# Long convolution and token mixing: the last 64 token rows in two column tiles of TensorE

## The chip, the cores and the metric

The kernel runs on one core of a Trainium2 chip. A core has five engines with their own instruction streams: TensorE (PE in the profile, its weight loads PEld), VectorE (DVE), ScalarE (ACT), GpSimd (POOL) and SyncE (SP). Data lies in HBM, in SBUF (128 partitions) and in PSUM, where TensorE puts its sums (128 partitions, eight banks of 512 float32 each). Transfers are issued from SP, ACT and POOL. The metric is the device time of one execution in microseconds (us), lower is better.

## What is computed

Two stages follow one another. The first is a long convolution of `x` (8 batches, 5696 tokens, 128 channels) with `h` along the tokens, by way of Fourier transforms. The second mixes tokens with two 5696 x 5696 matrices:

```python
x = irfft(rfft(x, n=2*S, axis=1) * rfft(h, n=2*S, axis=0), n=2*S, axis=1)[:, :S, :]
theta = x @ w_theta
zr, zi = x * cos(theta), x * sin(theta)
y = einsum('ts,bsd->btd', w_tok_r, zr) + einsum('ts,bsd->btd', w_tok_i, zi)
u = x + y
out = u + maximum(u @ w_ch, 0)
```

Batch and channel together are 1024 columns, so the mixing is a product of a 5696 x 11392 matrix (both weights side by side) with 11392 x 1024.

## The kernel before, in words

The first 570 us or so are the convolution, which doesn't change. What follows is the mixing.

**Tiles.** The 5696 token rows of the output are 44 tiles of 128 and one last tile of 64 (`NT - 1`, rows 5632 to 5695). The 1024 columns are two halves of 512, one PSUM bank each. The sum over 5696 input tokens is made in two passes (`p`), of 2816 tokens each (`H`), and 64 tokens left over, whose part is added in pass 1 by `zl` and `wl`. A pass takes its 2816 tokens in 11 blocks (`NJ`), each with a real and an imaginary half (`r`).

**Pairs and the seven products.** In a pass the 44 tiles go in pairs `tt` (tile `tt` with tile `22 + tt`). Most pairs are multiplied with Strassen's seven products, in banks `m0` to `m6` (named M2, M6, M7, M5, M1, M3, M4; line 1084 has the matmuls, line 1091 the adds on VectorE). For this, the z operand of each block `j` lies in SBUF as `bts[j]`, seven quarters of 512 columns: M2, M6, M7 and M5 begin as b11, b12, b21 and b22, and M3, M4, M1 (and M6, M7) become sums and differences of them (`sum_ops`, line 653, adds at line 655). The order of the pairs is 0 to 20, then the last tile alone (`None`), then 21 in pass 0, and 0, then the last tile, then 1 to 21 in pass 1. Pair 0 (and 1 in pass 0) is multiplied plainly (line 1005).

**The last tile.** It has 64 rows and can't be paired. Its product with b11, b12, b21, b22 is written in terms of the quarters that lie there:

```python
terms = ((sa, M2, a2, M4), (a1, M3, sa, M5))
```

`a1` and `a2` are the real and the imaginary weights of the tile, transposed, and `sa` their sum. Column half `h` = 0 is `sa` x quarter M2 plus `a2` x quarter M4; half 1 is `a1` x M3 plus `sa` x M5. For each block and `r` this makes four matmuls (lines 968 and 970), 128 deep, 64 rows out, 512 columns. Half 0 goes into one PSUM bank and half 1 into another, both on partitions 0 to 63.

**Stretches.** The 11 blocks are loaded in two chunks (6 and 5 blocks) and worked in four stretches of 3, 3, 3 and 2 blocks. For every stretch `prepare` transposes the weights on VectorE (line 714, into a pool of five buffers `wt`) and adds or subtracts them (line 723, into four buffers). It is called one stretch ahead. For the last tile a stretch needs two transposes and one sum.

**The ring of weights.** Weights come from HBM by transfers that POOL issues (line 509, four for each load) into a ring of six loads. A load may be issued when the load six places before it has been transposed to the end of its chunk.

**z between the passes.** Pass 1 needs other z blocks. `load_b` (line 639) reads them from `z_hbm`, two transfers for each block, issued on ACT, as soon as the block's buffer isn't needed by pass 0 any more; so these loads follow TensorE through pair 21. `start_pass(1)` then loads `zl` for the 64 left-over tokens (line 846, on SP) and adds its two halves (line 847).

**Sums and final stages.** In pass 0 the bank is added to an addend (`addend`: the convolution's output in bfloat16, `yy`, loaded on SP, line 826) and the float32 result stored to `cp_hbm` (`finish`, line 833). In pass 1 that is loaded again (line 828) and added (line 986 for the last tile), and `finish` appends a final stage (`u_stage`) to a list `spread`. Its first part copies to bfloat16 (line 791, ACT), transposes on TensorE (line 794, `utp`) and copies back (line 796); its second multiplies with `w_ch` (line 801, `v`), takes maximum and sum on VectorE (line 803) and stores to the output (line 805, SP). `aside` takes such stages from `spread` between the matmuls of later stretches, one in each stretch; in pass 1 also in the last tile's.

**What sets the order.** A scheduler orders most engines' instructions by data and buffers. From the start of pass 1 to its pair 1 (and from pair 0 to late in pair 2 of pass 0), VectorE keeps the order in which the code is written (`manual_schedule`, line 916). In the last tile's stretches of pass 1 that order is: transposes and sum of the next stretch, the final add of a `u_stage`, then three adds for each block (line 977).

Of the kernel before, what the change touches and what calls it, by code (L numbers as in the profile page):

```python
# [10 lines left out]
F32 = mybir.dt.float32  # L11
BF16 = mybir.dt.bfloat16
# [10 lines left out]
def kernel(  # L23
# [10 lines left out]
    nc = tc.nc  # L34
    B, S, D = x.shape
    assert D == 128
    P = 128
    NT = (S + P - 1) // P
# [12 lines left out]
    y2_hbm = y2_hbm_h.ap()  # L51
    cp_hbm = cp_hbm_h.ap()
# [66 lines left out]
    for p0, p1 in ((0, 80), (80, NB)):  # L119
        nc.gpsimd.dma_start(u_t[p0:p1, :N2 * D],  # L120
                            bass.AP(tensor=h.tensor, offset=h.offset + p0 * N2 * D,
                                    ap=[[N2 * D, p1 - p0], [1, N2 * D]]))
# [20 lines left out]
    def turns_of(pattern, base, lanes, m, per, quarter=None):  # L143

        n = 1
        for _, c in pattern:
            n *= c
        t = s2.tile([P, 11 * NB], F32, tag="turn", name="turn")[:m, :n]
        k = s2.tile([P, 11 * NB], F32, tag="whole", name="whole")[:m, :n]
        nc.gpsimd.iota(k, pattern=pattern, base=base, channel_multiplier=0,  # L150
                       allow_small_or_imprecise_dtypes=True)
        nc.gpsimd.tensor_scalar(t, k, lanes, 1.0 / per, op0=mult, op1=mult)
        if quarter is not None:
            quarter(t)
        nc.vector.tensor_scalar(k, t, MAGIC, None, op0=add)
        nc.vector.scalar_tensor_tensor(t, k, MAGIC, t, op0=ALU.subtract, op1=ALU.subtract)
        return t, k
# [12 lines left out]
    t, k = turns_of([[1, K1]], 0, lane[:NB, 1:2], NB, N1)  # L170
# [324 lines left out]
    def wl_room():  # L495
        ring["wl"] += 1
        return small((4 + ring["wl"] % 2) * P, P)

    def yt_room():
        return small(0, 4 * P).rearrange("p (b n) -> p b n", b=4)  # L500
# [59 lines left out]
    M2, M6, M7, M5, M1, M3, M4 = range(7)  # L560
# [92 lines left out]
    def sum_ops(bt):  # L653
        b11, b12, b21, b22 = (bt[q] for q in (M2, M6, M7, M5))
        return [lambda f=f, x=x: f(*x) for f, x in (  # L655
            (nc.vector.tensor_sub, (bt[M3], b12, b22)), (nc.vector.tensor_sub, (bt[M4], b21, b11)),
            (nc.vector.tensor_add, (bt[M1], b11, b22)), (nc.vector.tensor_add, (b12, b11, b12)),
            (nc.vector.tensor_add, (b21, b21, b22)))]
# [19 lines left out]
    mps = ctx.enter_context(tc.tile_pool(name="mps", bufs=1, space=bass.MemoryType.PSUM, reuse_waits="tile"))  # L678
# [29 lines left out]
    def half(z, ti, h):  # L708

        return z[ti].rearrange("p b d -> p (b d)")[:, h * 512:h * 512 + 512]  # L710
# [74 lines left out]
    def u_stage(ti, h, c, m):  # L785
        st = {}

        def first(tags=("misc", "misc", None)):
            st["tags"] = tags
            ub = ybp.tile([P, 4, D], BF16, tag="yb", name="ub")  # L790
            nc.scalar.activation(ub[:m].rearrange("p b d -> p (b d)"), c[:m], AF.Copy)  # L791
            utp = mps.tile([P, 4, P], BF16, tag=tags[0], name="utp")
            for b in range(4):
                nc.tensor.transpose(utp[:, b, :m], ub[:m, b, :], ident_bf[:m, :m])  # L794
            st["uts"] = uts = cp.tile([P, 4, P], BF16, tag=tags[2], name="uts") if tags[2] else yt_room()
            nc.scalar.activation(uts[:, :, :m], utp[:, :, :m], AF.Copy)  # L796

        def second():
            v = mps.tile([P, 512], F32, tag=st["tags"][1], name="v")
            for b in range(4):  # L800
                nc.tensor.matmul(v[:m, b * D:(b + 1) * D], st["uts"][:, b, :m], w_ch_sb,  # L801
                                 start=True, stop=True)
            nc.vector.scalar_tensor_tensor(c[:m], v[:m], 0.0, c[:m],
                                           op0=ALU.max, op1=ALU.add)
            nc.sync.dma_start(
                bass.AP(tensor=out.tensor, offset=out.offset + ti * P * D + 4 * h * S * D,
                        ap=[[D, m], [S * D, 4], [1, D]]),
                c[:m].rearrange("p (b d) -> p b d", b=4))
        return nothing, first, second

    tags, where_bg = {"n": 0}, {}

    def addend(p, k, ti, h, m=P):

        tag = f"c{k}"
        if p == 1:
            tag = ("c0", "c1", "c2", "c3", "red", "mag")[tags["n"] % 6]
            tags["n"] += 1
        c = cp.tile([P, 512], F32, tag=tag, name=f"c{k}")
        if p == 0 and ti in (22, 23):  # L820
            yT = cp.tile([P, 4, P], BF16, tag=f"yy{k}", name=f"yy{k}")
            nc.sync.dma_start(yT, yt_hbm[:, 4 * h:4 * h + 4, ti * P:ti * P + P])
            return c, yT
        if p == 0:
            yy = cp.tile([P, 512], BF16, tag=f"yy{k}", name=f"yy{k}")
            nc.sync.dma_start(yy[:m], half(y2_hbm, ti, h)[:m])
            return c, yy
        nc.sync.dma_start(c[:m], half(cp_hbm, ti, h)[:m])
        return c, c

    def finish(p, ti, h, c, m=P):
        if p == 0:
            nc.sync.dma_start(half(cp_hbm, ti, h)[:m], c[:m])
        else:
            spread.append(u_stage(ti, h, c, m))
# [78 lines left out]
    for i, (k, p, tt, j0, s0, nj) in enumerate(stretches):  # L914
# [17 lines left out]
        bts, zl = bts_of[p], zl_of[p]  # L932
# [7 lines left out]
        def aside(first_of, second_of):  # L940
            nonlocal second
            if first_of and spread and (p == 1 or (tt > 0 and not end_of_pair)):
                where_bg["tags"] = ("c2", "c3") if j0 + s0 == TJ else ("red", "mag")
                _, first, second = spread.pop(0)
                with tc.issue_after(sides["late"].ins) if p == 0 and tt == 1 else ExitStack():
                    first()
                    if len(spread) > 1:
                        spread[1][0]()
            if second_of and second is not None:
                second()  # L950
                second = None

        if tt is None:
            if p:
                aside(True, False)
            if first_of_pair:
                ps = [mps.tile([P, 512], F32, tag=f"m{q}", name=f"m{q}") for q in ((M1, M7) if p else (M3, M4))]
                cs = [addend(p, h, NT - 1, h, m=64) for h in range(2)]
            a1, a2, sa = a
            terms = ((sa, M2, a2, M4), (a1, M3, sa, M5))  # L960
            for j in range(nj):
                jj = j0 + s0 + j
                for r in range(2):
                    b = [x[:, r, :] for x in bts[jj]]
                    st_ = jj == 0 and r == 0
                    sp_ = jj == NJ - 1 and r == 1 and zl is None
                    for h, (x0, q0, x1, q1) in enumerate(terms):
                        nc.tensor.matmul(ps[h][:64], x0[:, j, :64, r], b[q0],  # L968
                                         start=st_, stop=False)
                        nc.tensor.matmul(ps[h][:64], x1[:, j, :64, r], b[q1],  # L970
                                         start=False, stop=sp_)
            if p:
                aside(False, True)
            if p == 1:
                for j in range(nj):
                    for op in sum_ops(bts[j0 + s0 + j])[2:]:
                        op()
            if end_of_pair:
                if zl is not None:
                    wl = wl_room()  # L980
                    nc.sync.dma_start(wl[:, :64], wl_hbm[:, NT - 1, :64])
                    for h in range(2):
                        nc.tensor.matmul(ps[h][:64], wl[:, :64], zl[h], start=False, stop=True)
                for h in range(2):
                    c, c0 = cs[h]
                    nc.vector.tensor_add(c[:64], c0[:64], ps[h][:64])
                    finish(p, NT - 1, h, c, m=64)
            continue
        classic = plain(p, tt)
        if first_of_pair and i:  # L990
# [1 line left out]
        if first_of_pair:  # L992
            where = ((tt, 1), (22 + tt, 0), (tt, 0), (22 + tt, 1))
            if zl is not None:
                wl = [wl_room(), wlp.tile([P, P], BF16, tag="wl1", name="wl1")]
                for n in range(2):
                    nc.sync.dma_start(wl[n], wl_hbm[:, 22 * n + tt, :])
        if j0 + s0 == (3 if classic else 2) * TJ:
            cs = (sides["cs"] if p == 0 and tt == 0 else
                  [addend(p, n, t, h) for n, (t, h) in enumerate(where)])  # L1000
# [33 lines left out]
        if classic:  # L1034
            for n in range(4):
# [4 lines left out]
                if end_of_pair and n % 2:  # L1040
                    (c12, z12), (c21, z21), (c11, z11), (c22, z22) = cs
                    out_of = (((c11, z11, 0), (c12, z12, 1)), ((c21, z21, 2), (c22, z22, 3)))[n // 2]
                    for h, (c, z, m_) in enumerate(out_of):
# [6 lines left out]
                        else:  # L1050
                            for b in range(4):
                                nc.tensor.matmul(ms[m_][:, b * D:(b + 1) * D], z[:, b, :], ident_bf,
                                                 start=False, stop=(b == 3))
# [11 lines left out]
        else:  # L1065
# [13 lines left out]
            for n, q in enumerate(ORDER):  # L1079
                sum_some(1)  # L1080
                for j in range(nj):
                    jj = j0 + s0 + j
                    for r in range(2):
                        nc.tensor.matmul(ms[q], a[q][:, j, :, r], bts[jj][q][:, r, :],  # L1084
                                         start=(jj == 0 and r == 0),
                                         stop=(jj == NJ - 1 and r == 1 and q not in left))
# [60 lines left out]
```

## Time and profile before

| | |
|---|---|
| median of 3 runs | 2110.66 us (2108.34 to 2111.68) |
| span of the profiled execution | 2116.2 us (nothing outside it is recorded) |
| busy in the span | PE 95%, DVE 76%, POOL 43%, ACT 32% |
| granted clock of TensorE, mean | 0.979 of full speed, 1.00 in the stretches of the last tile |
| last tile in pass 0 (lines 968, 970) | 1232.8 to 1251.8 us: 88 matmuls |
| pair 21, then start of pass 1 | from 1251.9 and from 1285.0 us |
| last tile in pass 1 | 1327.1 to 1351.2 us: 88 matmuls, 2 of line 983, three transposes `utp` and four products `v` of final stages |
| z of pass 1 read (line 639) | issued from 1259.0 to 1310 us, 8 to 19 us to landing |

The profile is one execution recorded instruction by instruction. Times count from the start of the span. A line of the timeline gives the start, the length, the engine, the code line, the operation, what it writes and reads, and in brackets how long the engine was idle before it and what ended that. Matmuls are pipelined: one of 512 columns is shown with 0.38 us, but the next can start 0.22 us after it, so the distance of starts is the cost of one in a row of many. "128\*64" is the part of the array in use: 128 rows deep, 64 columns.

### The profile page before, as it was taken

To read this page: it belongs to the slowest core of one execution; us is meant where nothing else is said; L and a number is where in the kernel's file an instruction comes from. 1 tells how busy PE (TensorE), PEld (TensorE's weight loads), DVE (VectorE), ACT (ScalarE), POOL (GpSimd) and SP (SyncE) were. 2 spreads that over 40 slices of the span, in tenths; PEclk is the share of its full clock that TensorE was granted. 3 is DMA by queue.
4 is the path that set the end of the run, shared out by engine and by line. 5 is a ranking of instruction groups with operands and counts; after the bars stand their busy time and mean duration, and the time that the engine had idled before them with its cause. 6 is when DMAs were issued, how large, how long until landed. Compare 5 with 4: busy or idle time off the path is not lost.

```text
span 2116.2 us, 41712 instructions
## 1 busy us (share of the span) xinstructions
PE 2008.1 (95%) x15873; PEld 1117.7 (53%) x15873; DVE 1598.3 (76%) x2884; ACT 673.9 (32%) x997; POOL 907.6 (43%) x1662
## 2 busy tenths in 40 slices
PE   4888999778999999999999999999999999999998
PEld 3788888654444444444444444444444444444444
DVE  7767776777778888888886755877777777776867
ACT  5778877774332333332310000111111111111111
POOL 5301010227444536354556543445454444545450
PEclk8799999999999999999999999999999999999999
DMA  6457474889989989898999879878888787979693
GB/s 140 98 130 170 117 180 127 216 245 243 178 153 179 176 176 168 170 176 173 174 165 156 142 137 296 128 117 147 140 143 145 134 153 128 156 127 157 124 156 90
DMA packets 408265, 334.97 MB, mean 158 GB/s; under 512 B 85927, under 2 KB 358439, under 8 KB 407079
## 3 DMA queue, kind: packets, MB, share of 16 engines
q0 software_dynamic: 225952, 156.72, 52.5%
q1 hardware_dynamic: 176128, 164.05, 27.3%
q10 hardware_dynamic: 5984, 11.54, 1.6%
q8 instruction: 124, 2.03, 0.4%
q14 instruction: 77, 0.63, 0.1%
HBM read 377.11 MB, written 92.49 MB: 222 GB/s over the span
## 4 chain that ended last, share of the span: by engine, by line
PE 68%; DMA 3%; DVE 3%; POOL 1%; issue 1%; ACT 0%; DVEq 0%; SPq 0%; POOLq 0%; ACTq 0%
PE m L1084 61%; PE m L1005 2%; DMA ring<-in_moe_w_tok_r_dram 1%; DMA b<-z_hbm 1%; POOL ring L509 1%; PE v L801 1%; PE utp L794 1%; DVE c L1091 1%; PE m L1088 1%; DVE b L655 1%; DVE wt L714 1%; DMA ring<-in_moe_w_tok_i_dram 0%; PE theta_ps L396 0%; PE tpz L742 0%; PE m L968 0%
## 5 line engine op out<-in xcount | busy, mean ns | idle before, releaser
L509 POOL DMA_DIRECT2D ring<-in_moe_w_tok_i_dram x720 | 387.9, 546 | 666.7 <-DVE wt L714 587.7
L714 DVE STREAM_TRANSPOSE wt<-ring 128x384 f32<-128x384 f32 (+2 forms) x720 | 360.5, 527 | 123.2 <-PE m L1084 71.3
L509 POOL DMA_DIRECT2D ring<-in_moe_w_tok_r_dram x720 | 386.4, 546 | 149.3 <-DVE wt L714 86.4
L1084 PE MATMUL m<-b,wt 128*128 128x512 bf16 x1640 | 388.3, 379 | 2.0 <-DVE wt L714 1.7
L1084 PEld LDWEIGHTS <-wt 128*128 128x128 bf16 x1804 | 175.8, 98 | 217.6 <-DVE wt L714 6.2
L1091 DVE TENSOR_TENSOR c<-c,m 128x512 f32<-128x512 f32 x412 | 266.9, 674 | 0.4 <-PE m L1084 0.4
L796 ACT ACTIVATE ring<-utp 128x512 bf16<-128x512 bf16 (+1 forms) x86 | 50.9, 592 | 586.2 <-PE utp L794 586.2
L328 PE MATMUL ps<-r_u,u_t 128*128 128x128 f16 x1024 | 128.6, 226 | 10.8 <-ACT red L419 5.6
L329 PE MATMUL ps<-r_v,v_t 128*128 128x128 f16 x1024 | 127.7, 226 | 0.4
L791 ACT ACTIVATE ub<-c 128x512 bf16<-128x512 f32 (+1 forms) x90 | 56.3, 628 | 215.0 <-DMA ring<-in_moe_w_tok_r_dram 123.8
L1005 PE MATMUL m<-b,wt 128*128 128x512 bf16 x480 | 112.9, 385 | 9.1 <-DVE wt L714 4.4
L130 POOL DMA_DIRECT2D x<-in_x_dram x64 | 33.9, 536 | 189.3 <-PE ps L194 177.8
L328 PEld LDWEIGHTS <-u_t 128*128 128x128 f16 x1024 | 104.1, 102 | 9.6 <-DVE u_t L312 6.2
L329 PEld LDWEIGHTS <-v_t 128*128 128x128 f16 x1024 | 103.4, 101 | 5.7 <-issue 3.2
L310 ACT ACTIVATE xs<-ps 128x1024 f16<-128x1024 f32 x96 | 95.9, 1023 | 15.1 <-DVE v_t L312 7.9
L312 DVE TENSOR_TENSOR u_t<-xs,hs 128x1024 f16<-128x1024 f16 x96 | 68.8, 716 | 32.1 <-ACT xs L310 19.7
L1005 PEld LDWEIGHTS <-wt 128*128 128x128 bf16 x528 | 50.8, 99 | 70.8 <-issue 8.7
L194 PE MATMUL ps<-f_t,x 89*128 89x180 f16 x512 | 77.2, 299 | 5.6 <-ACT xs L310 3.9
L212 PEld LDWEIGHTS <-w_t 64*128 64x128 f16 x3240 | 61.2, 102 | 34.8 <-issue 21.7
L398 ACT ACTIVATE red<-theta_ps,magic 128x512 f32<-128x512 f32 (+1 forms) x46 | 31.6, 687 | 133.7 <-PE theta_ps L396 116.0
L194 PEld LDWEIGHTS <-x 89*128 89x128 f16 x512 | 70.3, 241 | 6.6 <-issue 5.9
L744 ACT ACTIVATE ring<-tpz 128x512 bf16<-128x512 bf16 (+1 forms) x46 | 27.5, 597 | 132.6 <-PE tpz L742 108.9
(2914 smaller groups left out, 3916.7 us busy)
## 6 DMA issues: line engine op xcount, KB each, us to landing
ring<-in_moe_w_tok_r_dram POOLq DMA_DIRECT2D x352, 96.0 KB, 4.4
ring<-in_moe_w_tok_i_dram POOLq DMA_DIRECT2D x352, 96.0 KB, 5.0
ring<-in_moe_w_tok_r_dram POOLq DMA_DIRECT2D x352, 80.0 KB, 4.5
ring<-in_moe_w_tok_i_dram POOLq DMA_DIRECT2D x352, 80.0 KB, 3.9
hs<-hf_hbm SPq DMA_DIRECT2D x192, 128.0 KB, 3.2
cp_hbm<-c SPq DMA_DIRECT2D x88, 256.0 KB, 2.6
c<-cp_hbm SPq DMA_DIRECT2D x88, 256.0 KB, 4.4
out_dram<-c SPq DMA_DIRECT2D x88, 256.0 KB, 4.5
```

The costliest lines, as they stand in the source:

```text
L194: nc.tensor.matmul(ps[:, i // 2, (i % 2) * 2 * K1:(i % 2 + 1) * 2 * K1], lhs(q + i), f1_t[:NB], start=True, stop=True)
L212: nc.tensor.matmul(ps[:, e, j * HD:(j + 1) * HD], w_t2[rows, c0 + j, N2 * (1 - ri):N2 * (3 - ri)], a_st["a"][rows, ri * K1 + c0 + j, :], s ...
L310: nc.scalar.activation(xs[:, :, :, :ck], ps, AF.Copy)
L312: nc.vector.tensor_tensor(uv[r][:, :, :, c0:c0 + ck], xs[:, :, :, :ck], hv[:, r:r + 1, :, :ck].to_broadcast([P, 2, HD, ck]), op=mult)
L328: nc.tensor.matmul(o, u_t[:, at:at + P], r_u, start=True, stop=False)
L329: nc.tensor.matmul(o, v_t[:, at:at + P], r_v, start=False, stop=True)
L509: nc.gpsimd.dma_start(wb[32 * i:32 * i + 32, :ng, :nj * 64], bass.AP(tensor=a.tensor, offset=a.offset + row0 * S + p * H + i * QR + j0 * 6 ...
L714: nc.vector.transpose(wt.rearrange("p j t r -> p (j t r)").bitcast(F32).rearrange("p (j g t) -> p g j t", j=TJ, g=4)[:, :ng, :nj], wb[:, : ...
L791: nc.scalar.activation(ub[:m].rearrange("p b d -> p (b d)"), c[:m], AF.Copy)
L1005: nc.tensor.matmul(ms[n // 2 * 2 + h], a[n][:, j, :, r], bts_of[p][jj][n % 2 * 2 + h][:, r, :], start=(n % 2 == 0 and jj == 0 and r == 0), ...
L1084: nc.tensor.matmul(ms[q], a[q][:, j, :, r], bts[jj][q][:, r, :], start=(jj == 0 and r == 0), stop=(jj == NJ - 1 and r == 1 and q not in left))
L1091: nc.vector.tensor_tensor(c, z, ms[q], op=op)
```

## The change

The two column halves of the last tile go into one PSUM bank, half 0 on partitions 0 to 63 and half 1 on 64 to 127. TensorE then takes half 0's weights into its columns 0 to 63 and half 1's into 64 to 127. Matmuls of the two halves go by turns (first terms of both halves, then second terms). There is one accumulator, one addend `c_last`, one add of 128 partitions, and one store to `cp_hbm`, which uses the whole 128 rows of the last tile's place there (rows 64 to 127 hold half 1). In pass 1 one final stage of 128 partitions takes the place of two of 64; its result is stored by two transfers, one for each half.

```diff
@@ u_stage, second
-            nc.sync.dma_start(
-                bass.AP(tensor=out.tensor, offset=out.offset + ti * P * D + 4 * h * S * D,
-                        ap=[[D, m], [S * D, 4], [1, D]]),
-                c[:m].rearrange("p (b d) -> p b d", b=4))
+            for h_, p0, p1 in (((0, 0, 64), (1, 64, P)) if ti == NT - 1 else ((h, 0, m),)):
+                nc.sync.dma_start(
+                    bass.AP(tensor=out.tensor, offset=out.offset + ti * P * D + 4 * h_ * S * D,
+                            ap=[[D, p1 - p0], [S * D, 4], [1, D]]),
+                    c[p0:p1].rearrange("p (b d) -> p b d", b=4))
@@ new
+    def addend_last(p):
+        tag = "c0"
+        if p == 1:
+            tag = ("c0", "c1", "c2", "c3", "red", "mag")[tags["n"] % 6]
+            tags["n"] += 1
+        c = cp.tile([P, 512], F32, tag=tag, name="c_last")
+        if p == 0:
+            yy = cp.tile([P, 512], BF16, tag="yy0", name="yy_last")
+            for h in range(2):
+                nc.sync.dma_start(yy[64 * h:64 * h + 64], half(y2_hbm, NT - 1, h)[:64])
+            return c, yy
+        nc.sync.dma_start(c, half(cp_hbm, NT - 1, 0))
+        return c, c
@@ the last tile
-                ps = [mps.tile([P, 512], F32, tag=f"m{q}", name=f"m{q}") for q in ((M1, M7) if p else (M3, M4))]
-                cs = [addend(p, h, NT - 1, h, m=64) for h in range(2)]
+                q = M1 if p else M3
+                ps = mps.tile([P, 512], F32, tag=f"m{q}", name=f"m{q}")
+                c_last = addend_last(p)
...
-                    for h, (x0, q0, x1, q1) in enumerate(terms):
-                        nc.tensor.matmul(ps[h][:64], x0[:, j, :64, r], b[q0],
-                                         start=st_, stop=False)
-                        nc.tensor.matmul(ps[h][:64], x1[:, j, :64, r], b[q1],
-                                         start=False, stop=sp_)
+                    for k_ in range(2):
+                        for h, t in enumerate(terms):
+                            nc.tensor.matmul(ps[64 * h:64 * h + 64], t[2 * k_][:, j, :64, r], b[t[2 * k_ + 1]],
+                                             start=st_ and k_ == 0, stop=sp_ and k_ == 1)
...
-                        nc.tensor.matmul(ps[h][:64], wl[:, :64], zl[h], start=False, stop=True)
-                for h in range(2):
-                    c, c0 = cs[h]
-                    nc.vector.tensor_add(c[:64], c0[:64], ps[h][:64])
-                    finish(p, NT - 1, h, c, m=64)
+                        nc.tensor.matmul(ps[64 * h:64 * h + 64], wl[:, :64], zl[h], start=False, stop=True)
+                c, c0 = c_last
+                nc.vector.tensor_add(c, c0, ps)
+                finish(p, NT - 1, 0, c)
```

## The prediction

> **What bounds the kernel now.** I read the chain of waits on the page first, then the busy times of the two stretches in which the 64 rows are worked on, then the order of time inside them.
>
> ```profile
> PE 68%; DMA 3%; DVE 3%; POOL 1%; issue 1%; ACT 0%; DVEq 0%; SPq 0%; POOLq 0%; ACTq 0%
> 1232.80:1251.90 19.10, 19.10 (x90) 9.58 (x90) 7.53 (x19) 0.00 (x0) 8.57 (x16) 1.00 0.73 131
> 1327.00:1351.50 24.50, 23.36 (x122) 10.87 (x119) 22.89 (x44) 3.94 (x7) 9.36 (x18) 1.00 0.73 121
> ```
>
> The first line is the share of the chain by engine: TensorE (PE) holds 68% of what ended last. The other two are the stretches of pass 0 and pass 1 in which lines 968 and 970 run (columns after the length: PE, weight loads, VectorE (DVE), ScalarE, GpSimd (POOL), clock, DMA). In pass 0, PE is busy all 19.10 us and DVE 7.53: PE sets the end. In pass 1, DVE is busy 22.89 of 24.50 us: there PE has company, and the gain must be read from DVE.
>
> ```profile
> 1232.76 0.41 PE L968 MATMUL m<-ring,out__17787 128*64 128x512 bf16 x1
> 1232.78 0.11 PEld L970 LDWEIGHTS <-wt 128*64 128x64 bf16 x1
> 1233.00 0.38 PE L970 MATMUL m<-ring,wt 128*64 128x512 bf16 x1
> 1233.21 0.38 PE L968 MATMUL m<-ring,wt 128*64 128x512 bf16 x1
> ...
> 326.81 0.52 PEld L212 LDWEIGHTS <-w_t 64*128 64x128 f16 x32
> 326.81 0.64 PE L212 MATMUL ps<-a__6421,w_t 64*128 64x64 f16 x32
> ```
>
> Starts of matmuls lie 0.2157 us apart (88 from 1232.76 to 1251.74), whether or not they use half of the array's columns. A weight load of 64 columns (0.11 us) runs while a matmul streams. The last two lines are another stage, where matmuls go by turns to two halves of the array's rows: 32 of 64 columns in (0.64 - 0.19)/31 = 14.5 ns each. A full-array matmul of 128 columns comes every 56 ns in the same trace (line 328), so one of 64 would alone take some 28: two halves do work at once on this chip, with their loads. Two column halves are not in the trace.
>
> **The change, part by part.** Pass 0 and pass 1 each have 88 such matmuls, in stretches of 24, 24, 24 and 16. They become 44 pairs, one of each pair in array columns 0-63 and the other in 64-127. If a pair takes the time of one matmul, the four stretches take 12, 12, 12 and 8 x 0.2157 = 2.59, 2.59, 2.59 and 1.73 us instead of twice that. Bounds of a pair: 0.216 us (both at once, as L212) and 0.431 (by turns, as now); with both loads outside, 0.431 + 2 x 0.109 = 0.65. I take 0.216, the nearest row being L212.
>
> A rule of the Trainium skill ("TensorE: Matmul & The Clock Gate", Part 3, packing small matmuls) speaks against this: a weight load overlaps running matmuls only where the row group differs. Column halves share all rows, so by that rule a pair would take some 0.22 + 2 x 0.11 = 0.43 us and nothing would be won; the L970 load above, which starts 20 ns after a matmul in the same rows, speaks against it. The same part has three column tiles 2.38 times as fast as one after the other; as an estimate, two at that efficiency (0.79) would make a pair 0.27 us and take about 2 us from the gain below.
>
> *Pass 0.* What is late next is DVE:
>
> ```profile
> 1230.69 4.87 DVE L1091 TENSOR_TENSOR c<-c,m 128x512 f32<-128x512 f32 x8
> 1235.46 0.90 DVE L714 STREAM_TRANSPOSE wt<-ring 128x192 f32<-128x192 f32 x3
> 1236.28 0.32 DVE L723 TENSOR_TENSOR out__17845<-wt 128x384 bf16<-128x384 bf16 x1
> ```
>
> DVE adds the sums of the tile pair before until 1235.5, then transposes the weights of the second stretch and adds them (ready 1236.60). Today the first stretch lasts to 1237.9 and hides that. With 2.59 us it ends at 1235.35, and PE waits 1.3 us. Then 12 + 12 + 8 pairs: 1236.66 + 32 x 0.2157 = 1243.56, against 1251.74: **8.2 us** earlier. Later stretches find their weights: DVE's 4.4 us waits on L970 (for the five weight buffers) shrink, and it needs about 0.9 us for two transposes and a sum in each 2.59. The single sum of 128 rows comes ahead of w21's transpose in the order in which DVE's instructions are built, and the next pair's M3 bank waits for it: sum at 1243.8 to 1244.5 (0.67 us, row L986), while PE has four matmuls of M4 (0.86 us) first; if the next load of weights lands late (issued by POOL at 1236.1 to 1238.3, 4 to 5 us to landing), PE loses some 0.3. On SP one store of 128 rows takes the place of two of 64, and in pass 1 one load that of two: it has less to do, and nothing new is queued behind a wait there, since the two loads of the bf16 addend stay two and wait for the same buffer as before.
>
> The time won must pass through what follows. The next pair is PE's alone (1251.9 to 1285, no idle), then pass 1 needs z:
>
> ```profile
> 1250.00:1255.00 5.00, 5.00 (x24) 2.19 (x23) 3.46 (x7) 0.00 (x0) 0.00 (x0) 1.00 0.18 45
> 1255.00:1260.00 5.00, 5.00 (x25) 2.29 (x24) 3.65 (x9) 0.00 (x0) 3.98 (x8) 1.00 0.78 141
> 1265.00:1270.00 5.00, 5.00 (x25) 2.25 (x23) 2.84 (x6) 0.00 (x0) 2.71 (x5) 1.00 1.16 295
> 1290.00:1295.00 5.00, 5.00 (x25) 2.26 (x24) 0.09 (x1) 0.00 (x0) 0.00 (x0) 1.00 1.16 309
> ```
>
> DMA (share in the last column but one) is full, at 1.16, from 1265 to 1315, because z_hbm is read from 1259 on, as PE frees each b tile. PE then waits twice, 1.7 us at 1295 (zl, queued on SP behind b loads) and 1.2 at 1318. The b loads start 8 us earlier too. Does DMA have room? The 5 us shares from 1235 to 1315 sum to 15.9, so 79 us; at 1.16 that is 68 us of the 80. 11.7 us are free, mostly the hole at 1245 to 1260 that the earlier start closes. Four ring loads stay at 1236 to 1245 and may push into it. I take 0.5 us lost (bounds 0 and all 8.2, if b's landing did not move). Pass 0: 8.2 - 0.3 - 0.5 = **7.4 us**.
>
> *Pass 1.*
>
> ```profile
> 1331.09 0.36 DVE L723 TENSOR_TENSOR out__18603<-wt 128x384 bf16<-128x384 bf16 x1
> 1332.95 0.69 DVE L803 SCALAR_TENSOR_TENSOR c<-v,c 128x512 f32<-128x512 f32 x1 [1.50 <-PE v L801]
> 1340.51 5.50 DVE L655 TENSOR_TENSOR b<-b 128x1024 bf16<-128x1024 bf16 x9
> ...
> 1363.07 0.59 PE L1084 MATMUL m<-ring,out__18787 128*128 128x512 bf16 x2 [0.51 <-DVE c L986]
> ```
>
> DVE's order is fixed there. Each stretch costs it nine adds of b (5.5 us), two transposes and a sum (1.0) and a final add (0.69): 7.2 us, more than PE's 5.2. So halving PE wins one thing only: the final add at 1332.95 waits for v, behind the first stretch's matmuls; v will be there at 1330.5, and the add follows the sum at 1331.45: **1.5 us**. From there DVE runs without a gap to L986 at 1362.34. That sum then exists once instead of twice, and the built order puts six more matmuls ahead of the bank it frees: the 0.51 us wait goes. In the place of two final stages of 64 rows (utp 0.22 and v 0.34 each) comes one of 128 (0.22 + 0.22, as other pairs show): 1.12 - 0.44 = 0.68 us of PE. Pass 1: 1.5 + 0.5 + 0.7 = **2.7 us**; bounds 0 (if v is late for another reason) and 3.4 (0.67 us for the DVE sum on the path too). The two stores of 64 rows remain two and end 700 us before the kernel does.
>
> Sum: 7.4 + 2.7 = 10.1 us. The profiled span of 2116.2 becomes 2106.1. The runs' median is 5.5 us below that span, so I take the same off it: 2110.66 - 10.1 = **2100.6 us** (-0.48%).
>
> **Rivals.**
> - *By turns after all.* The two halves never overlap: a pair stays 0.431. For it: no row shows two column halves, and both read 128 rows of different moving data. Against it: L212. Left are the wait of 0.5 and the final stage's 0.7: 2109.4 us.
> - *Half hidden.* One load in each pair is exposed: 0.216 + 0.109 = 0.325 us. Pass 0 wins 44 x 0.106 = 4.7 (no DVE wait, since the first stretch then ends at 1236.66), less 0.5; pass 1 1.1 + 1.2: 2104.2 us. For it: the 64-column load takes 0.109, a full one 0.098. Against it: two such loads at 1232.75 and 1232.78 start 30 ns apart.
> - *Swallowed by DMA.* The pairs overlap, but b and zl land when they did, and pass 0 gives only what is left of the waits: 2110.66 - 2.7 = 2108.0 at the end of it; half of it, 2104.3. For it: 1.16 for 50 us. Against it: the hole before, and that the reads start when PE frees b.
> - *Slower: loads that stop the array.* If a load into one column half must wait until the other half's matmul is out, each of 88 matmuls pays 0.109 us: +9.6 us in pass 0, and in pass 1 PE (24.1 + 9.6) passes DVE, which sets that stretch now (7.2 x 3 + 5): about +7. 2110.66 + 16.6 - 1.2 = 2126 us. It decides from a pair above 0.46 us, where 44 x 0.03 eats the 1.2. For it: nothing shows a load beside a matmul in another column half. Against it: loads run beside matmuls everywhere else.
>
> **How the numbers follow.** Forecast 0.66, half hidden 0.10, swallowed 0.08, by turns 0.10, slower 0.06. The forecast's own range is 2097 (8.2 kept whole and 3.4, with 1.7 us of spread of the runs) to 2103.5 (2 us more lost in DMA, 1 in pass 1). To leave out no more than 2 in 10, I go up to 2107, past half hidden and half swallowed; by turns and slower stay out. 0.2% is 4.2 us, about what a measurement tells from no change: below 2106.4 is faster. Forecast, half hidden and a part of swallowed: 0.78; the rest of swallowed and by turns 0.15; slower 0.07.
>
> **What would show it.** In the profile after: pairs of matmuls starting some ns apart, the next pair 0.216 us later; 64-row stretch of pass 0 about 11 us long with one idle time of 1.3 us on DVE's sum; the first full-array matmul after it near 1243.7; z reads from about 1251; PE's waits near 1287 and 1310 no longer than 2 us; in pass 1 the stretch about 1.5 us shorter only, DVE at over 95%. Matmuls 0.216 apart would make it by turns; an unmoved zl landing, swallowed.

## The result, and the profile after

Over 20 runs the changed kernel took a median of **2102.05 us**, against 2111.72 us for the kernel before over 20 runs on the same chip: a ratio of **0.9954** (95% interval 0.9944 to 0.9964), or 9.7 us less (7.6 to 11.8). Forecast were 2100.6 us and 10.1 us less. The profiled run after took 2099.89 us with a span of 2098.1 us, 18.1 us below the span before; half of that difference is not the change, as the table of stretches below shows.

Pass 0 first: TensorE's order of time in the profile after, where the 64 rows begin (start, duration, engine, line, operation, output <- inputs, count, wait and who ended it).

```profile
1226.72 0.40 PE L986 MATMUL m<-ring,out__17787 128*64 128x512 bf16 x1
1226.72 0.62 PE L986 MATMUL m<-ring,wt 128*64 128x512 bf16 x2
1226.96 0.59 PE L986 MATMUL m<-ring,out__17787 128*64 128x512 bf16 x2
1227.18 0.59 PE L986 MATMUL m<-ring,wt 128*64 128x512 bf16 x2
...
1229.12 0.38 PE L986 MATMUL m<-b,out__17787 128*64 128x512 bf16 x1
1230.61 0.40 PE L986 MATMUL m<-b,out__17845 128*64 128x512 bf16 x1 [1.11 <-DVE out__17845 L723]
```

Lines 968 and 970 have become line 986. Matmuls now start in twos: two at 1226.72, then two in every 0.2157 us (1226.96, 1227.18; a line with x2 holds two, 0.2157 us apart). The stretch of 24 matmuls that took 5.2 us takes 2.6, and then TensorE waits for VectorE's sum: 1.11 us as listed, and 1.27 us from start to start beyond the usual 0.2157 (1229.12 to 1230.61), the wait that the prediction put at 1.3. The weight loads of the two halves stand in the same trace:

```profile
1226.71 0.11 PEld L986 LDWEIGHTS <-out__17787 128*64 128x64 bf16 x1 [0.42 <-DVE c L1106]
1226.72 0.14 PEld L986 LDWEIGHTS <-wt 128*64 128x64 bf16 x2
1226.75 0.32 PEld L986 LDWEIGHTS <-out__17787 128*64 128x64 bf16 x2
1226.96 0.32 PEld L986 LDWEIGHTS <-wt 128*64 128x64 bf16 x2
```

A load for one column half runs while the other half's matmul, which reads the same rows, is streaming. The rule that the prediction weighed against this (the Trainium skill, "TensorE: Matmul & The Clock Gate", Part 3: only a load into another row group overlaps, though the part elsewhere excepts a load into a background weight buffer) does not hold here. Busy times in the whole stretch (length; busy PE, weight loads, VectorE, ScalarE, GpSimd; granted clock; DMA share; GB/s):

```profile
1226.70:1237.60 10.90, 9.79 (x89) 4.88 (x88) 7.13 (x18) 0.00 (x0) 7.27 (x14) 1.00 0.89 178
```

19.10 us have become 10.90, with as many matmuls. VectorE does as much as before, so its share has gone from two fifths to two thirds.

In pass 1 it is VectorE that has to be read. Its order of time after the change:

```profile
1314.24 0.36 DVE L723 TENSOR_TENSOR out__18598<-wt 128x384 bf16<-128x384 bf16 x1
1314.52 0.68 DVE L803 SCALAR_TENSOR_TENSOR c<-v,c 128x512 f32<-128x512 f32 x1
1315.12 1.89 DVE L655 TENSOR_TENSOR ring<-ring 128x1024 bf16<-128x1024 bf16 x3
1316.92 3.69 DVE L655 TENSOR_TENSOR b<-b 128x1024 bf16<-128x1024 bf16 x6
```

The add of v (line 803) follows the weight sum at once: the wait of 1.50 us at 1332.95 is gone. The way from the last tile's first matmul to pair 1's first, before and after, in the view of busy times:

```profile
1327.14:1353.31 26.17, 23.27 (x120) 10.83 (x119) 24.57 (x47) 3.94 (x7) 9.22 (x18) 1.00 0.76 125
```

```profile
1310.30:1334.87 24.57, 15.30 (x120) 6.76 (x119) 24.47 (x47) 3.94 (x7) 9.31 (x18) 0.93 0.81 133
```

TensorE lost 8 of its 23 us, and the stretch lost 1.60: VectorE is busy 24.47 of 24.57. And the granted clock, 1.00 before, is 0.93. TensorE's waits and the clock around them, after:

```profile
1314.66 0.41 PE L986 MATMUL m<-b,out__18598 128*64 128x512 bf16 x1 [1.25 <-DVE out__18598 L723]
1321.61 0.63 PE L986 MATMUL m<-b,out__18655 128*64 128x512 bf16 x1 [3.18 <-DVE out__18655 L723]
1328.37 0.41 PE L986 MATMUL m<-b,out__18717 128*64 128x512 bf16 x1 [1.58 <-DVE out__18717 L723]
1335.24 0.63 PE L1099 MATMUL m<-ring,wt 128*128 128x512 bf16 x1 [3.63 <-DVE wt L714]
```

The last of these rows is not pair 1's first matmul: the trace lacks the record of that one, as it does in several runs, and of pair 21's first too. The weight loads show both, each with the load of a further matmul behind it:

```profile
1237.64 2.27 PEld L1099 LDWEIGHTS <-wt 128*128 128x128 bf16 x12 [0.41 <-DVE out__17950 L723]
1334.87 0.11 PEld L1099 LDWEIGHTS <-wt 128*128 128x128 bf16 x2 [3.55 <-DVE wt L714]
```

In the runs that have these two records, each stands within 0.02 us of its load (in the kernel before, 1251.87 and 1353.31 for both). So pair 1 starts at 1334.87, and the wait before it is 3.26 us, not 3.63.

```profile
1321.60:1325.00 3.40, 3.39 (x19) 1.36 (x20) 3.40 (x6) 0.60 (x1) 0.00 (x0) 0.54 0.46 133
1325.00:1328.30 3.30, 1.79 (x17) 0.78 (x13) 3.27 (x9) 0.00 (x0) 0.21 (x1) 1.00 0.29 79
1335.24:1338.60 3.36, 3.36 (x9) 1.30 (x9) 3.33 (x8) 0.00 (x0) 1.03 (x2) 0.54 0.19 59
1338.60:1342.00 3.40, 3.40 (x18) 1.51 (x17) 2.55 (x6) 0.00 (x0) 3.40 (x8) 1.00 1.03 125
```

Around the waits of 3.18 and 3.26 us the clock falls: it is 0.50 from 1321.29 to 1324.70 and from 1334.94 to 1338.35, 3.41 us each time (9 full-array matmuls are listed in 3.36 us, and 18 in the next 3.40). After those of 1.25 and 1.58 it does not fall.

All eleven profiles of this study by stretches, in us. "Start" is the first matmul of the 64 rows in pass 0; "64 rows, pass 0" goes from there to the first weight load of pair 21; "plain" from the first matmul of plain pair 0 in pass 1 to the first of the 64 rows; "64 rows, pass 1" from there to pair 1's first weight load. The other starts and ends are first matmuls in TensorE's order of time. (By first matmuls shown, five kernels with column tiles would have 11.15 or 11.16 us in pass 0 and the kernel after 24.94 in pass 1: that is the missing record and no time.)

| kernel | start | 64 rows, pass 0 | plain | 64 rows, pass 1 |
|---|---|---|---|---|
| before | 1232.76 | 19.11 | 41.97 | 26.17 |
| after | 1226.72 | 10.92 | 39.41 | 24.57 |
| column tiles in pass 0 only | 1230.07 | 10.92 | 40.39 | 26.17 |
| column tiles in pass 1 only | 1229.43 | 19.11 | 41.01 | 24.57 |
| one half after the other | 1222.01 | 13.66 | 40.69 | 25.34 |
| clock kept up | 1231.45 | 10.93 | 40.07 | 24.58 |
| 9 sums moved | 1225.89 | 10.92 | 40.20 | 21.63 |
| 18 sums moved | 1226.82 | 10.93 | 40.00 | 18.58 |
| kernel before, 18 sums moved | 1225.99 | 19.11 | 40.48 | 24.60 |
| 27 sums moved | 1225.56 | 10.92 | 39.75 | 14.48 |
| half 1 left out of pass 0 | 1227.72 | 10.92 | 42.12 | 24.57 |

The start varies from 1222.0 to 1232.8 although every kernel has the same code up to there: of the 18.1 us between the two spans, 6.0 come from it. The "plain" column varies by as much as 2.7 us, with the waits for late weights in it, and not with the change (39.4 to 42.1 with column tiles in pass 0, 40.5 to 42.0 without). The two stretches of 64 rows repeat within a few hundredths of a microsecond (10.92 or 10.93 in seven kernels; 24.57 or 24.58 in four). They are where this case can be read.

### The profile page after: what moved, and what is told of

Same layout as the page of the kernel before. It is cut to its first block, busy times and chain, and to the rows that moved or that the text cites. A ratio compares the mean times of both kernels' runs of the same rounds, so it can differ in the third digit from the quotient of the medians.

```text
span 2098.1 us, 41505 instructions
## 1 busy us (share of the span) xinstructions
PE 1979.5 (94%) x15688; PEld 1109.4 (53%) x15865; DVE 1595.2 (76%) x2881; ACT 675.3 (32%) x995; POOL 912.5 (43%) x1662
## 4 chain that ended last, share of the span: by engine, by line
PE 63%; DVE 4%; DMA 2%; issue 2%; POOL 0%; ACT 0%; DVEq 0%
PE m L1099 59%; DVE c L1106 2%; DMA ring<-in_moe_w_tok_r_dram 1%; DVE b L655 1%; PE v L801 1%; PE utp L794 1%; PE m L1103 1%; DVE wt L714 1%; PE tpz L742 0%; PE theta_ps L396 0%; POOL ring L509 0%; PE m L986 0%; DMA yT<-yt_hbm 0%; PE m L1020 0%; DMA zl<-zl_hbm 0%
## 5 line engine op out<-in xcount | busy, mean ns | idle before, releaser
L1099 PE MATMUL m<-b,wt 128*128 128x512 bf16 x1599 | 385.9, 380 | 4.1 <-DVE wt L714 1.7
L796 ACT ACTIVATE ring<-utp 128x512 bf16<-128x512 bf16 x85 | 50.8, 597 | 582.3 <-PE utp L794 582.3
L1020 PE MATMUL m<-b,wt 128*128 128x512 bf16 x466 | 110.2, 381 | 8.9 <-DMA b<-z_hbm 4.9
L791 ACT ACTIVATE ub<-c 128x512 bf16<-128x512 f32 x88 | 55.0, 628 | 191.5 <-DMA ring<-in_moe_w_tok_r_dram 113.0
L212 PEld LDWEIGHTS <-w_t 64*128 64x128 f16 x3240 | 60.8, 102 | 37.5 <-issue 24.5
```

What stands on the lines that cost most here:

```text
L212: nc.tensor.matmul(ps[:, e, j * HD:(j + 1) * HD], w_t2[rows, c0 + j, N2 * (1 - ri):N2 * (3 - ri)], a_st["a"][rows, ri * K1 + c0 + j, :], s ...
L1020: nc.tensor.matmul(ms[n // 2 * 2 + h], a[n][:, j, :, r], bts_of[p][jj][n % 2 * 2 + h][:, r, :], start=(n % 2 == 0 and jj == 0 and r == 0), ...
```

## The experiments

**Each pass alone.** The places in which the new form is chosen were made to depend on the pass; the first is shown, and matmuls, sums, loads and stores follow it:

```diff
-                q = M1 if p else M3
-                ps = mps.tile([P, 512], F32, ...)
+                if p == 0:        # in the second run: p == 1
+                    q = M1 if p else M3
+                    ps = mps.tile([P, 512], F32, ...)
+                    c_last = addend_last(p)
+                else:
+                    ps = [mps.tile(...) for q in ((M1, M7) if p else (M3, M4))]
+                    cs = [addend(p, h, NT - 1, h, m=64) for h in range(2)]
```

> Column tiles in pass 0 only; pass 1 works the last tile as the kernel before. Theory (pass 0 gives nearly all, because PE alone sets that stretch): 88 matmuls in about 10.9 us as in the changed kernel, 8 us won there, and all of it or a little more (the waits at the start of pass 1) kept: 8 to 10 us under the kernel before, ratio 0.9955 to 0.9965. Rival (both passes give alike, as both have the same 88 matmuls): 5 us, ratio 0.9975.

> Column tiles in pass 1 only. Theory (DVE sets that stretch, so only the 1.5 us wait for v and half a final stage can go): 1 to 3 us under the kernel before, ratio 0.9987 to 0.9995; the stretch of the last tile 1 to 2 us shorter, PE idle in it, clock below 1.00 in some slices of it as in the changed kernel. Rival (alike): 5 us, ratio 0.9975. If the two waits of PE at the start of pass 1 (1.7 and 1.2 us) are gone here too, their going has nothing to do with pass 0.

Pass 0 alone took 2104.35 us, ratio 0.9959 (0.9945 to 0.9973); pass 1 alone 2111.01, ratio 0.9990 (0.9976 to 1.0005), which can't be told from no change. In us below the kernel before: 8.7 (5.7 to 11.6) and 2.1 (-1.1 to 5.1), together 10.8 where the change has 9.7. These go by the ratios; the medians alone (2111.35 for the kernel before on that chip) differ by 7.0 and 0.3. The stretches don't depend on that choice: 8.2 us shorter in the one, 1.6 in the other. Most of the gain is pass 0.

**One half after the other.** In each stretch all matmuls of half 0 come first, then all of half 1; bank, sum and final stage stay those of the change.

```diff
-            for j in range(nj):
...
+            for h, t in enumerate(terms):
+                for j in range(nj):
...
-                    for k_ in range(2):
-                        for h, t in enumerate(terms):
+                        for k_ in range(2):
```

> The changed kernel's bank, sum, addend, stores and final stage, but in each stretch all matmuls of column half 0 and then all of half 1, so that two neighbours seldom lie in different halves. Theory (the gain is the two halves at work at once): pairs gone, the last tile in pass 0 takes some 18.5 to 19 us again, ratio 0.999 to 1.000. Rival (the gain is from one bank, one sum and one final stage, or from the order of transfers): ratio stays at 0.9954.

2102.94 us, ratio 0.9960 (0.9945 to 0.9975). By the theory this kernel should have lost the gain of pass 0, and it kept most of it. Nor is that the gain of one bank, one sum and one final stage without any overlap, for TensorE's order of time in that run shows the halves overlapping still:

```profile
1222.01 0.41 PE L986 MATMUL m<-ring,out__17787 128*64 128x512 bf16 x1
...
1223.54 0.38 PE L986 MATMUL m<-b,wt 128*64 128x512 bf16 x1
1223.76 0.38 PE L986 MATMUL m<-b,out__17787 128*64 128x512 bf16 x1
1223.77 0.40 PE L986 MATMUL m<-ring,wt 128*64 128x512 bf16 x1
1223.97 0.38 PE L986 MATMUL m<-b,wt 128*64 128x512 bf16 x1
1224.01 0.38 PE L986 MATMUL m<-ring,out__17787 128*64 128x512 bf16 x1
```

The matmul at 1223.77 reads "ring", the first block: it is half 1's first, thirteenth in the program, and it starts beside half 0's ninth. The stretch took 13.66 us: 5.4 below 19.11, where four overlapping matmuls at each of the seven changes of half in four stretches would give 7 x 4 x 0.2157 = 6.0. So taking turns is not what makes two column halves run together. It makes them do so all the time: 10.92 us.

**Half 1 left out.** In pass 0, 43 of half 1's 44 matmuls are left out; the kernel's output for these rows lacks them.

```diff
                         for h, t in enumerate(terms):
+                            if p == 0 and h and not (st_ and k_ == 0):
+                                continue
```

> The changed kernel with half 1 left out of the last tile's sum in pass 0, but for its first matmul: 44 matmuls and one in place of 88, all in one column tile (its output is not the reference's there). Theory (the second column tile costs nothing beside the first): the stretch from the first of these matmuls to pair 21's first stays at 10.9 to 11.2 us, with the matmuls 0.216 us apart. Rival (the two column tiles hinder one another a little): 0.3 to 2 us shorter than 10.9.

The stretch's busy times in that run:

```profile
1227.70:1238.85 11.15, 9.89 (x46) 4.79 (x47) 7.25 (x19) 0.00 (x0) 7.59 (x15) 1.00 0.89 177
```

From the first matmul to pair 21's first weight load it is 10.92 us, as with both halves. Beside half 0, half 1's 43 matmuls cost nothing that shows in a hundredth of a microsecond. (This was one execution.)

**The clock kept up.** To ask whether the fallen clock is what pass 1's gain went into, matmuls into an unused bank were put in after each stretch of pass 1.

```diff
+            if p == 1:
+                if first_of_pair:
+                    ps_w = mps.tile([P, 512], F32, tag=f"m{M7}", name="ps_w")
+                for n in range((6, 14, 6, 12)[(j0 + s0) // 3]):
+                    nc.tensor.matmul(ps_w, w_ch_sb, bts[10][M2][:, 0, :], start=True, stop=True)
```

> The changed kernel with 38 further full matmuls in pass 1, into a free bank and read by nobody, in PE's idle times between the last tile's stretches. Theory (PE's clock went to half because it was idle 3 us at a time, and that cost part of pass 1's gain): clock 1.00 in all slices of that stretch and of the first 5 us of pair 1; pair 1's first 12 matmuls 0.22 us apart instead of 0.43; from the start of the last tile in pass 1 to the first matmul of zl in pair 1 some 1 us less than the 56.8 us of the changed kernel. Rival (the slow clock lies under DVE's time and costs nothing): the same 56.8 us with the clock at 1.00.

One run, 2105.17 us, with a span of 2103.4 that started the 64 rows 4.7 us later than the change's; its stretch of pass 1 is what tells:

```profile
1315.70:1340.28 24.58, 21.97 (x158) 9.82 (x157) 24.48 (x47) 3.94 (x7) 9.28 (x18) 0.99 0.78 133
```

With TensorE busy and the clock at 0.99, the stretch is 24.58 us against 24.57: the clock was worth nothing there, and VectorE, busy 24.48 us, set it, as the rival said. A wait of 2.61 us before pair 1 remained and the clock was at 0.50 after it, so what the clock costs in pair 1 was not tested by this run: its way from the 64 rows to pair 1's first matmul on `zl` was 56.65 us, against 56.81 after the change and some 1 us less expected.

The run with half 1 left out of pass 0 has the same code in pass 1 as the change, the same 24.57 us and the same wait of 3.26 us before pair 1 (3.49 as listed, its first matmul missing). There the clock did not fall behind that wait:

```profile
1338.59:1342.00 3.41, 3.18 (x15) 1.58 (x17) 3.38 (x8) 0.00 (x0) 0.71 (x2) 1.00 0.33 93
1348.75 0.61 PE L1101 MATMUL m<-ring,out__18736 128*128 128x512 bf16 x2 [0.70 <-DVE c_last L1003]
```

Its way to the first matmul on `zl` is 55.78 us, 1.03 less than after the change, and all of it in pair 1 (31.20 us from the first weight load, against 32.24). So the fallen clock cost the change 1.0 us in pair 1. The second line says why it is not more: with the clock up, TensorE waits 0.70 us for the bank that `c_last` frees. In the kernel after, 3.41 us at half the clock make TensorE some 1.7 us late (half of 3.41), and it finds that bank free. The run with nine sums moved, below, also has the clock at 1.00 there: 31.20 us again, with a wait of 0.69 for the bank.

**VectorE's sums moved.** If VectorE sets pass 1, then sums taken from it there should bring what halving TensorE could not. Line 655 does three sums for each of eleven b blocks in these stretches, 27 of them during the 64 rows and six in pair 1, though only pair 1 needs their results, and VectorE waited 5.82 and 5.17 us during plain pair 0. First nine of them (blocks 0 to 2) go there, then nine more (blocks 3 to 5); a third run does the latter to the kernel before.

```diff
+    def early(n):
+        if n == 1:
+            for j in range(TJ):
+                for op in sum_ops(bts_of[1][j])[2:]:
+                    op()
+        if n == 4:                      # not in the run with 9
+            for j in range(TJ, 2 * TJ):
+                for op in sum_ops(bts_of[1][j])[:3]:
+                    op()
...
             for n in range(6):
                 some(n)
+                if p == 1 and j0 + s0 == 2 * TJ:
+                    early(n)
...
-                for j in range(nj):
+                for j in range(nj if j0 + s0 >= 2 * TJ else 0):
                     for op in sum_ops(bts[j0 + s0 + j])[2:]:
...
-                    for op in sum_ops(bts[j0 + s0 + j])[:2]:
+                    for op in sum_ops(bts[j0 + s0 + j])[slice(3, 5) if j0 + s0 == TJ else slice(2)]:
```

> Theory (VectorE sets the length of the last tile in pass 1): the nine sums that overwrite or fill operands of blocks 0 to 2 (9 x 0.61 = 5.5 us) leave the last tile's stretches and run where VectorE waited 5.82 us for TensorE near 1286. The way from the last tile's first matmul to pair 1's first (24.94 us in the changed kernel, 26.17 before) falls to about 19.5, and the time to about 0.9928 of the kernel before (2096.5 us). Rival A (the lowered clock and TensorE's own waits set it): no gain, 24.5 to 25 us and 0.9954 as the changed kernel. Rival B (VectorE is not free near 1286, the sums delay the weights of the next stretch): the last tile falls by 5.5 but plain pair 0 grows by as much, 0.995.

> The same with blocks 3 to 5 too: 18 sums (11 us) leave the last tile's stretches in pass 1. Theory: VectorE has 24.9 - 11.0 = 13.9 us left there, TensorE has 44 x 0.216 + 3.3 + 0.6 = 13.4, so the way to pair 1's first matmul is 15 to 16 us; plain pair 0 may grow by 0 to 2 us. Time about 0.991 of the kernel before (0.990 to 0.9925), which beats the changed kernel by some 9 us. Rival A (clock and TensorE's waits): 0.9954. Rival B (the sums only move the wait into plain pair 0): 0.994 to 0.9955.

> The kernel before with the same 18 sums moved, column tiles nowhere. Theory: there TensorE has 88 x 0.2157 + 3.3 + 0.6 = 22.9 us in the last tile of pass 1, so of 26.17 us at most 3.3 can go: about 0.9985 of the kernel before (0.9975 to 0.9995). The column tiles in pass 1 are then worth 7 us once VectorE is out of the way, and 1.2 while it is not. Rival (the sums moved early are worth the same whatever TensorE does): 9 to 11 us here too, 0.995 to 0.996.

| | median us | ratio (95%) | 64 rows, pass 1 |
|---|---|---|---|
| change, 9 sums moved | 2096.89 | 0.9933 (0.9912 to 0.9953) | 21.63 |
| change, 18 sums moved | 2094.19 | 0.9921 (0.9909 to 0.9934) | 18.58 |
| before, 18 sums moved | 2109.03 | 0.9990 (0.9978 to 1.0002) | 24.60 |

The three times came close to the theory's 0.9928, 0.991 (with an edge at 0.9925) and 0.9985. By itself the run with nine does not decide: its interval reaches to 0.9953, and its stretch of 21.63 us lies between the theory's 19.5 and rival A's 24.5; "plain", at 40.20, did not grow by the 5.5 us of rival B. The other two decide. The same move is worth 6.0 us of that stretch where TensorE has column tiles and 1.6 where it has not; the other way round, column tiles in pass 1 are worth 1.6 us while VectorE has all its sums and 6.0 once 18 are gone. The stretches fell by 2.9 and 6.0 us where the theory had 5.5 and 9 to 10, though, and VectorE's order of time in the run with 18 says why:

```profile
1319.23 0.69 DVE L803 SCALAR_TENSOR_TENSOR c<-v,c 128x512 f32<-128x512 f32 x1 [2.40 <-PE v L801]
...
1322.93 0.69 DVE L803 SCALAR_TENSOR_TENSOR c<-v,c 128x512 f32<-128x512 f32 x1 [2.27 <-PE v L801]
1323.54 5.50 DVE L655 TENSOR_TENSOR b<-b 128x1024 bf16<-128x1024 bf16 x9
1328.96 1.49 DVE L714 STREAM_TRANSPOSE wt<-ring 128x384 f32<-128x384 f32 x3
```

VectorE now waits for v, twice, with work left that could fill the waits: nine sums of blocks 6 to 8 stand behind them, and pair 1's first transposes behind those. TensorE waited 3.58 us for these transposes (3.81 as listed, with the first matmul missing).

**27 sums moved.** So four of those nine go ahead of the first of these adds of v, five ahead of the second.

```diff
             if p:
+                fill = [o for j in range(2 * TJ, 3 * TJ) for o in sum_ops(bts[j])[2:]]
+                for op in {TJ: fill[:4], 2 * TJ: fill[4:]}.get(j0 + s0, ()):
+                    op()
                 aside(False, True)
```

> The run with 18 sums moved, and the nine sums of blocks 6 to 8 as well: four of them go before the add of v in the second stretch and five before that in the third, where VectorE waited 2.40 and 2.27 us for v. Theory (VectorE's queue, up to the transposes for pair 1, sets the end of the last tile): the transposes come about 4.7 us earlier (they started at 1328.96, TensorE waited 3.81 us for them), so the way from the last tile's first matmul to pair 1's falls from 18.8 to 15 us and the time to about 0.9905 of the kernel before (0.9895 to 0.992). Rival (a sum delays the weights of the third and fourth stretch instead, or pair 1 gives the time back): 18 to 19 us again, 0.992.

**2090.56 us, ratio 0.9903 (0.9885 to 0.9921)**: the best of the study, 11 us below the change. The stretch and the start of pair 1, in TensorE's order of time and in busy times:

```profile
1324.20 0.38 PE L1114 MATMUL m<-ring,wt 128*128 128x512 bf16 x1 [0.16 <-DVE wt L714]
```

```profile
1309.49:1323.97 14.48, 13.24 (x116) 6.27 (x114) 14.38 (x30) 3.51 (x7) 9.21 (x18) 1.00 0.97 150
1324.20:1355.30 31.10, 30.94 (x150) 14.19 (x153) 23.69 (x48) 1.43 (x3) 17.15 (x32) 1.00 1.02 171
```

The first weight load of pair 1 is at 1323.97, so the stretch is 14.48 us where 15 were expected, with both engines nearly full (13.24 and 14.38 us), hardly any wait before pair 1, and the clock at 1.00 throughout.

## Why the prediction was right, and which terms were not

- **A pair takes the time of one matmul: right.** 0.2157 us for each pair, two starts some ns apart, and the kernel with half 1 left out took as long as that with it. The rivals "by turns after all" and "half hidden" fall with the 10.92 us of the stretch: half hidden would have made it 44 x 0.325 = 14.3. "Slower" needed a load that stops the array; the loads ran beside the other half's matmuls.
- **Pass 0's 8.2 us, less 1.3 for VectorE's sum already in it: right.** 19.11 to 10.92 is 8.19; the wait was 1.27 from start to start. (The 1251.74 of the prediction is where the last of 88 steps of 0.2157 ends; the last matmul starts at 1251.56.) The 0.3 us for a late bank is not seen: the way from pair 21's first weight load to plain pair 0's first matmul is 33.30 us before and 33.25 after.
- **0.5 us lost in DMA: not seen, nor excluded.** The "plain" stretch, where a loss would stand, varies by 2.7 us among profiles of the same code. The two waits that the prediction has at 1.7 and 1.2 us are 1.17 us each in the trace before (at 1296.86 and 1319.04). After the change they were gone, but the half-left-out kernel, with the same early start, had two waits again (1.29 and 1.17). "Swallowed by DMA" falls: pass 0 alone kept 7.0 us (medians) to 8.7 us (ratio) to the end.
- **Pass 1's 2.7 us: the first term right, the bank's wrong, and the clock left out.** The 1.5 us for the add of v came as 1.60: the wait went. The other two terms, 0.5 for the bank and 0.7 for one final stage, were to show in pair 1. There the prediction missed what TensorE's longer waits do to its clock: from pair 1's first weight load to its first matmul on `zl` it took 32.02 us before and 32.24 after, 0.2 more and not 1.2 less. With the clock up (half 1 left out of pass 0) it took 31.20. Of that gain of 0.8, the bank has no part: the wait for it was to go and was 0.70 us instead of 0.51. Six more matmuls were to stand ahead of it, but the trace has 43 in pair 1 ahead of it where the kernel before has 42. The rest, 0.8 + 0.2 = 1.0, is left for the one final stage, more than its 0.7; only 0.45 of it shows in the stage's own matmuls (1.13 to 0.68 us in pair 1). So pass 1 is worth 2.4 us with the clock up (58.19 to 55.78 us from the 64 rows to that matmul), and 1.4 with the clock as it fell (56.81).

Summed, 8.2 + 1.6 - 0.2 = 9.6 us from the two stretches and pair 1, against 9.7 (7.6 to 11.8) over the runs. That the forecast's 10.1 is so near is in part luck: the 0.8 us taken off for DMA and the bank in pass 0 did not show, and the 1.3 us by which pass 1's term was too large made up for it.

Reading the forecast's signs: the first full-array weight load at 1237.64 and z's first read at 1244.98 are both 6 us ahead of the 1243.7 and 1251 foretold, as the start of that execution is (6.04 us).

## What to carry to other kernels

Two small matmuls in two column halves of the array run in the time of one even when they read the same rows, and taking turns in the program keeps them together; but what it is worth is what the other engine of that stretch allows: 8 us where VectorE was two fifths busy, 1.6 where it was full. After halving one engine's work, look at once at the next engine's queue for work that is done early without need; here the second step, moving VectorE's sums into its waits, brought more (11 us) than the first. And compare two executions stretch by stretch, between marks that repeat: in this kernel 6 of the 18 us between two spans arose before the changed code. Check a mark against the weight loads before reading tenths from it: a first matmul without a record made stretches look 0.2 to 0.4 us longer here.

## What the runs showed of the hardware

- **Two column halves run ahead of each other.** With half 1's matmuls written behind all of half 0's, its first started while half 0's ninth of twelve did (1223.77 and 1223.76), so some four matmuls ahead of its place in the program.
- **The clock fell at waits of 2.6 us and more, though not at each.** TensorE's waits of 2.58, 2.61, 3.18, 3.19, 3.26 (twice), 3.30 and 3.58 us in pass 1 came with 3.41 us at a granted clock of 0.50 (6.83 us at the one of 3.19), which began between 1.1 us before the next matmul and 0.7 after it; those of 1.85 us or less came with none. In the kernel with half 1 left out, a wait of 3.18 us was followed by the low clock only 1.4 us after the next matmul, and one of 3.26 by none. The Trainium skill ("TensorE: Matmul & The Clock Gate", Part 1) has the clock fall to half after an idle window of about 3.4 us that runs free of the program; the half clock and its 3.41 us agree with the rows, and so does it that equal waits end differently, but 2.58 us of listed wait were enough here.
